# A lead of 52 instead of 48 row maxima in a fused Fourier mixing and attention kernel

## The chip, the cores and the metric

The kernel runs on one core of a Trainium2 chip. The metric is device time in microseconds (us) of one execution. The core's engines run side by side, each on its own instruction stream: PE (TensorE) does the matmuls, DVE (VectorE), ACT (ScalarE) and POOL (GpSimd) do the element work, SP's queue issues most transfers. They meet through semaphores only.

## The reference

The input x has 2048 rows (S) of 512 (D). Two branches are mixed row by row by a gate:

```python
g = _sigmoid((x * gate_w).sum(-1, keepdims=True))
# branch a: real part of a two-dimensional DFT, as dense matrices
a = jnp.einsum("bsd,ed->bse", x, dft_hid_re)
b = jnp.einsum("bsd,ed->bse", x, dft_hid_im)
y = jnp.einsum("ts,bse->bte", dft_seq_re, a) - jnp.einsum("ts,bse->bte", dft_seq_im, b)
# branch b: attention with H = 32 heads of 16
q, k, v = qkv[0], qkv[1], qkv[2]
scores = jnp.einsum("bhqd,bhkd->bhqk", q, k) * scale
p = _softmax(scores, axis=-1)
o = jnp.einsum("bhqk,bhkd->bhqd", p, v)      # then o @ wo
return g * y + (1 - g) * (o @ wo)
```

All is float32. Products that need the precision are made of three: each operand is split into a high and a low part, and high x high, high x low and low x high are summed.

## The kernel before

**Two halves of PE.** Most operands have at most 64 rows of contraction, so the kernel keeps the upper and the lower 64 rows of the array busy with two different matmuls at a time. A *slot* is one such place in the order: one matmul on either half.

**The softmax needs row maxima first.** Heads are handled in 16 pairs; head 0 of a pair lives in rows 0 to 63 of the stacks `qs` and `ks`, head 1 in rows 64 to 127. Each stack exists twice, and pair p uses number p % 2. `load_stacks(p)` (L202 to L211) fills the two stacks of a pair from DRAM by twelve DMAs of 128 KB in SP's queue, the six of head 0 first. A *maxima tile* (`a_tile`, L217) multiplies 128 query rows with 512 keys (L223), and DVE reduces the result to one maximum per row (L225). A pair has 64 such tiles per head. When a block of them is complete, `m_parts` and `m_rows` (L233, L242) split the negated maxima and write them by eight small DMAs (L248, four from SP and four from POOL) into two further rows of `qs`. A *score* (`scores`, L727) then multiplies 50 rows (L741), so that the maximum is subtracted by the matmul itself, and ACT takes the exponential (L742). `pv` (L767) multiplies the result with the values (L777) for two units (a unit is 128 keys of one pair and half of the queries).

**The maxima run ahead of the scores.** The distance is `LEAD` (L26), 48 tile indices for each head. It is built before the scores begin. `four` (L307) makes the products of four row tiles at a time for V and for the imaginary part of the hidden DFT; it has four phases of twelve product slots, and after the slots 3 and 8 of each phase it adds a pair of maxima tiles, one per head (L323, `maxima`).

**The long middle stage** is a written order of *sections*. A section is one string of slots and ends with `|`, the value matmuls of two units. In a string `s` is a score, `a` a maxima tile, both on one half, while the other half gets a product of the DFT (L429); a two-letter slot has a score or tile on both halves and no product. Head 1's first letters stand in the even sections, head 0's in the odd ones. 24 sections are THIN, 192 are FULL (16 slots, eight scores and eight maxima tiles). The last 32 sections with the output projection as the other work are FOURTEEN (8 pairs of sections), NINE (3), TEN, TWELVE, TEN, TWELVE, TEN; their names and what they hold:

```python
FULL = "s a s s a a s s a a s a s a a s |"
NINE = "aS s a s a ^ sA a a s a s sA |", "aS a s s a ^ sA a s a s s aS sA |"
FOURTEEN = "s a s a sS ^ a s s a s a aA |", "aS s a a s ^ s a sS s a s a sA |"
TWELVE = ("sA a s a s ^ s a s a s s a s |",) * 2
TEN = "aA s s a s ^ s s s a a sS |", "a s a sS a ^ s s s s s aA |"
```

A pair of sections holds 16 maxima tiles in NINE, 14 in FOURTEEN, 12 in TWELVE, 10 in TEN. `^` and the end of a section take one deferred step of the maxima.

**What sets the order of the loads.** Transfers that don't belong to a DFT chain are called by a plan (`at`, `run_plan`) at the end of a section by the number of units whose values are done: `load_stacks(p)` at unit 32 (p - 1) - 1, when the last scores that read the same buffers, pair p - 2's, have just been issued. In SP's queue stand, among others, the chunks of the DFT matrix (`craw`, L364), the row of a finished chain (`yr`, L483), the blocks of attention output (`oh<-nh`, L570, which waits for POOL) and these loads (L210, L211), in the order of the program.

**The first rows** of the real part are made by `four` too, while the first scores are taken (L971 to L983); `real_next` (L443) copies each of four results to a tile `y`, of which there are two. **The start** has eight matmuls on zeros (L157 to L160) before the first loads arrive. **The end**: `LastPair.products` (L688) makes the last four row blocks; block 0 is finished by ACT and POOL, the others by DVE (L609), and each is stored by one DMA (L700).

Of the kernel before, what the change touches and what calls it, by code (L numbers as in the profile page):

```python
# [22 lines left out]
KT = D // P  # L23
NT = S // P
UNITS = NP * 32
LEAD = 48  # L26
RAW = 6
PSUM = bass.MemoryType.PSUM
DRAM = bass.MemoryType.DRAM
# [3 lines left out]
def mix_kernel(ctx: ExitStack, tc: tile.TileContext, xa_t, xa, wqkv, w_hid, w_seq, wo, gate_w, out):  # L33
# [5 lines left out]
    nc = tc.nc  # L39
# [5 lines left out]
    const = ctx.enter_context(tc.tile_pool(name="const", bufs=1))  # L45
# [10 lines left out]
    oh_d = [[dram.tile([P, 2, S // 2], F32, name=f"oh{hf}{ct}") for ct in range(3)] for hf in range(2)]  # L56
    r_d = [[dram.tile([2, 4, S // 2], F32, name=f"r{hf}{ct}") for ct in range(4)] for hf in range(2)]

    ident = const.tile([P, P], F32, name="ident")
    make_identity(nc, ident)  # L60

# [5 lines left out]
    omg = const.tile([P, NT], F32, name="omg")  # L67
# [5 lines left out]
    xab = [const.tile([P, 4, 2, D], F32R, name=f"xab{tb}", tag=f"xab{tb}") for tb in range(4)]  # L73
# [22 lines left out]
    wch = st1.tile([P, KT, D], F32R, name="wch")  # L96
    wcl = st1.tile([P, KT, D], F32R, name="wcl")
# [32 lines left out]
    with tc.tile_pool(name="qk", bufs=1, reuse_waits="tile") as pool:  # L130
        wh = pool.tile([P, 2, KT, D], F32R, name="wh")
        wl = pool.tile([P, 2, KT, D], F32R, name="wl")

        def mm_qk(ps, c, ct, tb, kt):
            cols = slice(ct * P, (ct + 1) * P)
            x = xab[tb][:, :, :, kt * P:(kt + 1) * P]
            mm3(ps, wh[:, c, kt, cols], wl[:, c, kt, cols], x[:, :, 0], x[:, :, 1], kt == 0, kt == KT - 1)

        def evac_qk(ps, c, ct, tb):
            hl = pool.tile([P, 2, D], F32R, name="hl", bufs=7)  # L140
            hi_lo(hl[:, 0], hl[:, 1], ps)
            nc.sync.dma_start(qk_d[c][:, ct * P:(ct + 1) * P, tb * 512:(tb + 1) * 512].rearrange("v p t -> p v t"),
                              hl.bitcast(F32))

        for kt in range(KT):
            add(wh[:, 0, kt], wl[:, 0, kt], wqkv[0, :, kt], nc.vector)
            add_x(0, kt)
        for kt in range(KT):
            add(wh[:, 1, kt], wl[:, 1, kt], wqkv[1, :, kt], nc.vector)
        for tb in range(1, 4):  # L150
            for kt in range(KT):
                add_x(tb, kt)
        for kt in range(KT):
# [3 lines left out]
        nc.vector.memset(wch[:, 0].bitcast(F32), 0.0)  # L157
        ps = turn_of("f")
        for _ in range(8):
            nc.tensor.matmul(ps, wch[:, 0, :P], wch[:, 0], start=True, stop=True)  # L160
        split(8)

        xgs = {}

        def gate_row(s):

            xg = xgs.pop(s)
            nc.vector.scalar_tensor_tensor(xg, xg, 1.0, gwb, op0=ALU.mult, op1=ALU.mult, accum_out=z[:, s:s + 1])
            if s + 5 < NT:
                xgs[s + 5] = staged(xa[s + 5])  # L170

        for tb in range(4):
            if tb == 2:
                assert not todo and not loaded
                nc.sync.dma_start(gwb, gate_w.broadcast_to([P, D]))
                xgs.update({s: staged(xa[s]) for s in range(5)})
            for c in range(2):
                if tb == 0 and c == 0:
                    pss = [turn_of("f") for _ in range(4)]
                    for kt in range(KT):  # L180
                        for ct in range(4):
                            mm_qk(pss[ct], c, ct, tb, kt)
                    split(4)
                    for ct in range(4):
# [83 lines left out]
    ab = [xab[s // 4][:, s % 4] for s in range(NT)]  # L268
# [35 lines left out]
        a_next += 1  # L304
        return users[1]

    def four(ss, wh, wl, done, between=None):  # L307

        ps = [turn_of("s") for _ in ss]
        seen = None  # L310
        for phase, pair in enumerate(((0, 1), (2, 3), (1, 0), (3, 2))):
            guard, seen = seen, None
            both = [row_products(ss[c], wh, wl) for c in pair]
            for j in range(12):
                for half, c in enumerate(pair):
                    st, mv = next(both[half])
                    r = slice(64 * half, 64 * half + 64)
                    i = nc.tensor.matmul(ps[c], st[r], mv[r], start=phase < 2 and j == 0, stop=phase > 1 and j == 11)  # L318
                    if phase > 1 and j == 0:
                        tc.add_manual_dep(  # L320
                            i.ins, guard.ins.name,
                            mybir.DependencyInfo(mybir.DependencyClass.Sync, mybir.DependencyReason.DATA))
                if j in (3, 8):  # L323
                    user = between(phase, j) if between else maxima()
                    seen = seen or user
            if deferred:
                deferred.pop(0)()
            if phase > 1:
                for c in sorted(pair):
                    done(ss[c], ps[c])  # L330

    for s in range(8):
        ps = turn_of("s")
# [11 lines left out]

    wre = [[const.tile([P, D], F32R, name=f"wre{v}{kt}", tag=f"w{4 * v + kt}") for kt in range(KT)] for v in range(2)]
    for s in range(0, NT, 4):
        four(range(s, s + 4), [wch[:, kt] for kt in range(KT)], [wcl[:, kt] for kt in range(KT)], b_done)
    run_deferred()
    assert a_next == LEAD  # L350
    right.__exit__(None, None, None)
# [88 lines left out]
                yield chain, h1, wre[1][kt], None  # L440
                yield chain, l1, wre[0][kt], partial(real_next, s, t, chain) if kt == KT - 1 else None

    def real_next(s, t, chain):  # L443
        y = work.tile([P, D], F32, name="y", bufs=2)
        nc.scalar.copy(y, chain.ps)  # L445
# [52 lines left out]
    oh, yp, wos = {}, {}, []  # L498
# [100 lines left out]

    few, by_others = [], set()  # L600

    def finish(ps, t, y, other=False):
        if other:

            tmp = few[0][:, t % 4]
            nc.scalar.activation(tmp, ps, AF.Copy, scale=omg[:, t:t + 1])
            nc.gpsimd.tensor_tensor(y, y, tmp, ALU.add)
            return
        nc.vector.scalar_tensor_tensor(y, ps, omg[:, t:t + 1], y, op0=ALU.mult, op1=ALU.add)  # L609

# [41 lines left out]
    class LastPair:  # L652
# [35 lines left out]
        def products(self, others):  # L688

            pss = [o_bank() for _ in range(4)]  # L690
            for i, (st, mv) in enumerate(((0, 0), (0, 1), (1, 0))):
                for c in range(4):
                    r = slice(32 * c, 32 * c + 32)
                    nc.tensor.matmul(pss[c], self.o15[r, st], w15[0][r, mv], start=i == 0, stop=i == 2)
            for c in sorted(range(4), key=lambda c: c not in others):
                t = 8 + 4 * self.blk + c
                finish(pss[c], t, yp[t], c in others)
            for c in range(4):
                t = 8 + 4 * self.blk + c
                (nc.scalar if c in others else nc.sync).dma_start(out[t * P:(t + 1) * P, :], yp.pop(t))  # L700

    last_pairs = []

# [169 lines left out]

    FULL = "s a s s a a s s a a s a s a a s |"
    THIN = "aS s a s a s s a s a s a a sA |"
    NINE = "aS s a s a ^ sA a a s a s sA |", "aS a s s a ^ sA a s a s s aS sA |"
# [91 lines left out]
    run_plan(0)  # L968
    gate()

    def first_rows(s, ps):  # L971
# [72 lines left out]
```

## Time and profile before

| what | value |
|---|---|
| median of 3 runs | 1681.99 us (1681.66 to 1682.1) |
| profiled execution, its own time | 1682.39 us |
| its span, first to last instruction | 1680.6 us |
| mean granted TensorE clock | 0.999 |
| 345 to 1450 us (THIN's end and FULL): busy PE, DVE, ACT, POOL | 1104.99, 952.77, 883.19, 562.21 of 1105.00 |
| 1456 to 1577 us (FOURTEEN and NINE) | 120.69, 105.87, 100.08, 32.27 of 121.00 |
| 1577 to 1640 us (TEN and TWELVE) | 62.80, 49.93, 55.98, 22.85 of 63.00 |

The profile belongs to one execution, so sums of its rows are compared with that execution's own time, 1682.39 us. A matmul's length in it runs until its result has left the array; neighbours overlap, and the pace is the distance between starts. L777 counts 16 matmuls at a section's end, since each of the eight of the program is recorded as two.

### The profile page before, as it was taken

How to read it: one execution, taken by the hardware profiler on the slowest of the kernel's cores; microseconds unless marked ns; L12 is line 12 of the kernel's file. 1: busy time of each engine (PE TensorE's matmuls, PEld its weight loads, DVE VectorE, ACT ScalarE, POOL GpSimd, SP SyncE). 2: the span in 40 equal slices, each digit the busy share in tenths (PEclk: the TensorE clock that was granted, in tenths of full speed). 3: DMA queues.
4: the chain of work that ended last, by engine and by line, in shares of the span. 5: the costliest groups of instructions: out<-in, count | busy, mean ns of one | idle time of the engine just before them, and what ended most of it. 6: DMA issues, size and time to landing. Idle time of an engine off the chain costs nothing.

```text
span 1680.6 us, 34603 instructions
## 1 busy us (share of the span) xinstructions
PE 1670.8 (99%) x13120; PEld 1016.6 (60%) x13120; DVE 1378.1 (82%) x2297; ACT 1245.8 (74%) x2469; POOL 750.9 (45%) x813
## 2 busy tenths in 40 slices
PE   9999999999999999999999999999999999999998
PEld 7888766655555555555555555555555555555554
DVE  5448688888888888888888888888888888888885
ACT  5212288877777888778877788777877788788886
POOL 0214634544444466445444466454554465322231
PEclk9999999999999999999999999999999999999999
DMA  9963500314141432414165533423241535731014
GB/s 294 341 155 108 178 13 14 52 45 83 45 84 46 83 101 85 83 46 89 39 145 190 103 108 89 96 55 73 64 89 46 103 102 108 273 66 34 26 40 134
DMA packets 82622, 165.16 MB, mean 98 GB/s; under 512 B 19904, under 2 KB 20168, under 8 KB 78616
## 3 DMA queue, kind: packets, MB, share of 16 engines
q1 hardware_dynamic: 77832, 162.30, 37.2%
q8 instruction: 103, 1.69, 0.4%
q0 software_dynamic: 4480, 0.39, 0.3%
q14 instruction: 63, 0.52, 0.1%
q10 hardware_dynamic: 144, 0.26, 0.0%
HBM read 107.73 MB, written 54.52 MB: 97 GB/s over the span
## 4 chain that ended last, share of the span: by engine, by line
PE 98%; POOL 1%; DVE 1%; issue 0%; DMA 0%; SPq 0%; ACT 0%; DVEq 0%; POOLq 0%; ACTq 0%
PE d L429 40%; PE t L777 27%; PE t L223 11%; PE t L741 7%; PE t L318 4%; PE t L90 2%; PE t L89 2%; PE t L91 2%; PE t L336 1%; PE t L758 1%; PE t L429 1%; DVE mx L225 0%; PE d L223 0%; PE t L160 0%; POOL hl L295 0%
## 5 line engine op out<-in xcount | busy, mean ns | idle before, releaser
L225 DVE TENSOR_REDUCE mx<-t 128x1 f32<-128x512 f32 x2022 | 1255.6, 684 | 211.1 <-PE t L223 173.4
L742 ACT ACTIVATE pt<-t 128x512 f32<-128x512 f32 x2048 | 1034.1, 629 | 10.1 <-PE t L741 9.9
L741 PE MATMUL t<-qs,ks 50*128 50x512 f32 x2048 | 741.6, 409 | 0.8 <-ACT y L445 0.5
L223 PE MATMUL t<-ks,qs 48*128 48x512 f32 x2022 | 690.4, 400 | 0.1
L429 PE MATMUL d<-xab,ch 64*128 64x512 f32 x2016 | 657.5, 401 | 0.0
L777 PE MATMUL t<-pt,vt 128*32 128x512 f32 x3968 | 477.1, 598 | 0.2
L429 PEld LDWEIGHTS d<-xab,ch 64*128 64x128 f32 x2016 | 357.7, 184 | 132.9 <-issue 98.9
L223 PEld LDWEIGHTS t<-ks,qs 48*128 48x128 f32 x2022 | 367.7, 185 | 80.2 <-ACT pt L742 42.0
L741 PEld LDWEIGHTS t<-qs,ks 50*128 50x128 f32 x2048 | 370.4, 185 | 67.1 <-DVE mx L225 37.9
L429 PE MATMUL d<-xab,cl 64*128 64x512 f32 x1008 | 403.6, 400 | 0.0
L792 POOL TENSOR_TENSOR osum<-osum,oe 128x512 f32<-128x512 f32 x217 | 279.7, 1289 | 161.0 <-ACT oe L786 154.1
L786 ACT COPY oe<-t 128x512 f32<-128x512 f32 x217 | 127.5, 588 | 230.6 <-PE t L777 228.2
L777 PEld LDWEIGHTS t<-pt,vt 128*32 128x32 f32 x3968 | 103.8, 109 | 231.2 <-issue 148.4
L374 POOL CAST ch<-craw 128x512 fp32r<-128x512 f32 x126 | 77.4, 615 | 351.4 <-PE t L741 291.6
L429 PEld LDWEIGHTS d<-xab,cl 64*128 64x128 f32 x1008 | 185.7, 184 | 67.8 <-issue 51.1
L375 POOL TENSOR_TENSOR cl<-craw,ch 128x512 fp32r<-128x512 f32 x126 | 162.5, 1290 | 10.2
L248 POOL DMA_DIRECT2D qs<-mt x132 | 74.3, 568 | 77.7 <-DVE mt L244 72.6
L429 PE MATMUL d<-wo_hl,o_hl 64*128 64x512 f32 x288 | 77.3, 395 | 0.0
L429 PE MATMUL d<-wre,xab 64*128 64x512 f32 x288 | 70.4, 389 | 0.0
L429 PEld LDWEIGHTS d<-wo_hl,o_hl 64*128 64x128 f32 x288 | 52.2, 185 | 13.4 <-DVE yp L609 5.0
L429 PEld LDWEIGHTS d<-wre,xab 64*128 64x128 f32 x288 | 52.9, 185 | 3.9 <-DVE mx L225 0.3
L89 PE MATMUL t<-xab,wh 128*128 128x512 f32 x128 | 50.2, 392 | 0.0
(123 smaller groups left out, 913.1 us busy)
## 6 DMA issues: line engine op xcount, KB each, us to landing
craw<-w_seq SPq DMA_DIRECT2D x128, 256.0 KB
qk<-hl SPq DMA_DIRECT2D x32, 512.0 KB
qs<-qk SPq DMA_DIRECT2D x96, 128.0 KB
ks<-qk SPq DMA_DIRECT2D x96, 128.0 KB
b<-hl SPq DMA_DIRECT2D x16, 512.0 KB
xab<-b SPq DMA_DIRECT2D x16, 512.0 KB
o<-osum SPq DMA_DIRECT2D x62, 128.0 KB
oh<-nh SPq DMA_DIRECT2D x12, 512.0 KB
```

The costliest lines, as they stand in the source:

```text
L89: nc.tensor.matmul(ps, sh, mh, start=first, stop=False)
L223: nc.tensor.matmul(ps, qs[p % 2][r, qt * P:(qt + 1) * P], ks[p % 2][r, kb * 512:(kb + 1) * 512], start=True, stop=True)
L225: user = nc.vector.tensor_reduce(mx[p % 2][:, h, qt, kb:kb + 1], ps, AX.X, ALU.max)
L248: (nc.sync, nc.gpsimd)[h].dma_start(rows.rearrange("v (q b c) -> v b q c", q=n, b=4)[:, b], mt[k % 2][32 * b + h:32 * b + 4 * n:2])
L374: nc.gpsimd.tensor_copy(h1, raw)
L375: nc.gpsimd.tensor_tensor(l1, raw, h1.bitcast(F32), ALU.subtract)
L429: i = nc.tensor.matmul(self.ps, st[r], mv[r], start=not self.begun, stop=stop)
L741: nc.tensor.matmul(ps, ks[p % 2][rr, kt * P:(kt + 1) * P], qs[p % 2][rr, q0:q0 + 512], start=True, stop=True)
L742: return nc.scalar.activation(pts[u][:, 2 * qb + h], ps, AF.Exp, bias=0.0, scale=DH ** -0.5)
L777: nc.tensor.matmul(acc[32 * j:32 * j + 32], vt[:, kt, p, h:h + 32], pt[:, j], start=u == us[0], stop=u == us[-1])
L786: nc.scalar.copy(oe, acc)
L792: nc.gpsimd.tensor_tensor(o, o, oe, ALU.add)
```

## The change

`LEAD` is 52. In the four groups of the imaginary rows, one phase of each (the second) has three pairs of maxima tiles instead of two. Every maxima tile of the later stream stands four indices earlier, beside the same scores. The late sections hold eight tiles fewer: NINE is gone, and there are FOURTEEN (11 pairs of sections), TEN (3), TWELVE, TEN. Four smaller edits: the matmuls on zeros read a tile of their own, set before anything else on DVE, and are ten; the first twelve products are ordered by operand (high x high of all four, then the low weights, then the low x); the four `y` of the first rows have four places; the last row block is finished and stored in two halves, by two queues, and block 0's ACT and POOL work is cut in two.

```diff
-LEAD = 48
+LEAD = 52
...
+    zero = const.tile([P, P], F32R, name="zero", tag="zero")
+    nc.vector.memset(zero.bitcast(F32), 0.0)
     ident = const.tile([P, P], F32, name="ident")
...
-        nc.vector.memset(wch[:, 0].bitcast(F32), 0.0)
         ps = turn_of("f")
-        for _ in range(8):
-            nc.tensor.matmul(ps, wch[:, 0, :P], wch[:, 0], start=True, stop=True)
+        for _ in range(10):
+            nc.tensor.matmul(ps, zero, zero.unsqueeze(1).broadcast_to([P, 4, P]), start=True, stop=True)
...
-                    for kt in range(KT):
+                    for w, v in ((wh, 0), (wl, 0), (wh, 1)):
+                        for ct in range(4):
+                            nc.tensor.matmul(pss[ct], w[:, c, 0, ct * P:(ct + 1) * P], xab[tb][:, :, v, :P],
+                                             start=w is wh and not v, stop=False)
+                    for kt in range(1, KT):
...
-                if j in (3, 8):
+                if j in ((2, 5, 9) if three and phase == 1 else (3, 8)):
...
-        four(range(s, s + 4), [wch[:, kt] for kt in range(KT)], [wcl[:, kt] for kt in range(KT)], b_done)
+        four(range(s, s + 4), [wch[:, kt] for kt in range(KT)], [wcl[:, kt] for kt in range(KT)], b_done, three=True)
...
-    def real_next(s, t, chain):
-        y = work.tile([P, D], F32, name="y", bufs=2)
+    def real_next(s, t, chain, y=None):
+        if y is None:
+            y = work.tile([P, D], F32, name="y", bufs=2)
...
-            tmp = few[0][:, t % 4]
-            nc.scalar.activation(tmp, ps, AF.Copy, scale=omg[:, t:t + 1])
-            nc.gpsimd.tensor_tensor(y, y, tmp, ALU.add)
+            for c in range(n):
+                cols = slice(c * D // n, (c + 1) * D // n)
+                tmp = few[0][:, t % 4, cols]
+                nc.scalar.activation(tmp, ps[:, cols], AF.Copy, scale=omg[:, t:t + 1])
+                nc.gpsimd.tensor_tensor(y[:, cols], y[:, cols], tmp, ALU.add)
...
-                finish(pss[c], t, yp[t], c in others)
+                halves = [slice(0, D // 2), slice(D // 2, D)] if self.blk and c == 3 else [slice(0, D)]
+                for cols in halves:
+                    finish(pss[c][:, cols], t, yp[t][:, cols], c in others, 2)
...
-        for patterns, n in ((FOURTEEN, 8), (NINE, 3), (TEN, 1), (TWELVE, 1), (TEN, 1), (TWELVE, 1), (TEN, 1)):
+        for patterns, n in ((FOURTEEN, 11), (TEN, 3), (TWELVE, 1), (TEN, 1)):
...
-        real_next(s, ab[s], chain)
+        if s % 2 == 0:
+            first_y.append(work.tile([P, 2, D], F32, name="y01", tag=("no", "nh")[s // 2]))
+        real_next(s, ab[s], chain, first_y[-1][:, s % 2])
```

The lines of the changed kernel are a few higher: L223, L429, L741 and L777 are L228, L434, L756 and L792 there.

**Where the stream of maxima reaches the stacks of pair 10.** This is PE's order before, inside the even section that follows the value matmuls at 1049.64 us of the profile (L223 is a maxima tile of head 1, L741 a score, L429 a DFT product; `qs1` and `ks1` are pair 9's stacks, `qs0` and `ks0` pair 10's):

```order
L223 MATMUL t_14730<-ks1_937,qs1_935 128x512
L429 MATMUL d_14534<-xab2_177,ch_14498 128x512
L223 MATMUL t_14734<-ks1_937,qs1_935 128x512
L429 MATMUL d_14534<-xab2_177,ch_14498 128x512
L741 MATMUL t_14738<-qs1_935,ks1_937 128x512
L429 MATMUL d_14534<-xab2_177,cl_14499 128x512
L223 MATMUL t_14742<-ks1_937,qs1_935 128x512
```

and this is the same place of the changed kernel:

```order
L228 MATMUL t_14755<-ks1_940,qs1_938 128x512
L434 MATMUL d_14559<-xab2_179,ch_14523 128x512
L228 MATMUL t_14759<-ks0_939,qs0_937 128x512
L434 MATMUL d_14559<-xab2_179,ch_14523 128x512
L756 MATMUL t_14763<-qs1_938,ks1_940 128x512
L434 MATMUL d_14559<-xab2_179,cl_14524 128x512
L228 MATMUL t_14767<-ks0_939,qs0_937 128x512
```

The fifth maxima tile of the section is the first that reads pair 10's stacks; before, head 1 came to them two sections later, after its first score there. The section with the call of the loads is the same in both, three sections ahead. So it is for each pair from 1 to 14.

**A phase of the imaginary rows.** PE's order before, from the first slots of the second phase of the first group (L318 is a product, x2 and x4 are one and two slots on both halves; L223 a maxima tile):

```order
L318 MATMUL t<-wcl,xab_175 128x512 x2
L318 MATMUL t<-wch,xab_175 128x512 x4
L223 MATMUL t<-ks_936,qs_934 128x512 x2
L318 MATMUL t<-wcl,xab_175 128x512 x2
L318 MATMUL t<-wch,xab_175 128x512 x4
L318 MATMUL t<-wcl,xab_175 128x512 x2
L318 MATMUL t<-wch,xab_175 128x512 x2
L223 MATMUL t<-ks_936,qs_934 128x512
L223 MATMUL d<-ks_936,qs_934 128x512
```

and in the changed kernel:

```order
L323 MATMUL t<-wcl,xab_177 128x512 x2
L323 MATMUL t<-wch,xab_177 128x512 x2
L228 MATMUL t<-ks_939,qs_937 128x512 x2
L323 MATMUL t<-wch,xab_177 128x512 x2
L323 MATMUL t<-wcl,xab_177 128x512 x2
L323 MATMUL t<-wch,xab_177 128x512 x2
L228 MATMUL t<-ks_939,qs_937 128x512
L228 MATMUL d<-ks_939,qs_937 128x512
L323 MATMUL t<-wch,xab_177 128x512 x2
L323 MATMUL t<-wcl,xab_177 128x512 x2
L323 MATMUL t<-wch,xab_177 128x512 x4
L228 MATMUL t<-ks_939,qs_937 128x512 x2
```

The phase has a third pair of maxima tiles, and so one slot more.

More of the change, by code (lines that the diff above doesn't have):

```diff
@@ L305, in maxima, with four @@
         return users[1]
-    def four(ss, wh, wl, done, between=None):
+    def four(ss, wh, wl, done, between=None, three=False):
         ps = [turn_of("s") for _ in ss]
@@ L600, in mix_kernel, with finish @@
     few, by_others = [], set()
-    def finish(ps, t, y, other=False):
+    def finish(ps, t, y, other=False, n=1):
         if other:
-            tmp = few[0][:, t % 4]
-            nc.scalar.activation(tmp, ps, AF.Copy, scale=omg[:, t:t + 1])
-            nc.gpsimd.tensor_tensor(y, y, tmp, ALU.add)
+            for c in range(n):
[3 more added lines that the diff above has]
+                nc.gpsimd.tensor_tensor(y[:, cols], y[:, cols], tmp, ALU.add)
             return
@@ L696, in products @@
                 t = 8 + 4 * self.blk + c
-                finish(pss[c], t, yp[t], c in others)
+                halves = [slice(0, D // 2), slice(D // 2, D)] if self.blk and c == 3 else [slice(0, D)]
+                for cols in halves:
+                    finish(pss[c][:, cols], t, yp[t][:, cols], c in others, 2)
             for c in range(4):
                 t = 8 + 4 * self.blk + c
-                (nc.scalar if c in others else nc.sync).dma_start(out[t * P:(t + 1) * P, :], yp.pop(t))
+                y = yp.pop(t)
+                if self.blk and c == 3:
+                    nc.scalar.dma_start(out[t * P:(t + 1) * P, :D // 2], y[:, :D // 2])
+                    nc.sync.dma_start(out[t * P:(t + 1) * P, D // 2:], y[:, D // 2:])
+                else:
+                    (nc.scalar if c in others else nc.sync).dma_start(out[t * P:(t + 1) * P, :], y)
     last_pairs = []
@@ L875, in mix_kernel @@
     THIN = "aS s a s a s s a s a s a a sA |"
-    NINE = "aS s a s a ^ sA a a s a s sA |", "aS a s s a ^ sA a s a s s aS sA |"
     FOURTEEN = "s a s a sS ^ a s s a s a aA |", "aS s a a s ^ s a sS s a s a sA |"
@@ L969, in mix_kernel @@
     gate()
+    first_y = []
     def first_rows(s, ps):
```

## The prediction

> **What bounds the kernel now.** I read the page's busy times and chain of waits first, then PE's timeline in the long middle stage, then the timeline of SP's queue beside it.
>
> ```profile
> PE 1670.8 (99%) x13120; PEld 1016.6 (60%) x13120; DVE 1378.1 (82%) x2297; ACT 1245.8 (74%) x2469; POOL 750.9 (45%) x813
> PE 98%; POOL 1%; DVE 1%; issue 0%; DMA 0%; SPq 0%; ACT 0%; DVEq 0%; POOLq 0%; ACTq 0%
> ```
>
> PE is busy for 99% of the span and carries 98% of the chain. It takes its matmuls in program order, so every microsecond for which one of them waits in the middle stage is added to the end; there is no idle time in which it could be won back. So the question is whether the change makes a matmul wait. Pair 10 shows where to look:
>
> ```profile
> 1049.64 1.92 PE L777 MATMUL t<-pt,vt 128*32 128x512 f32 x16
> ...
> 1053.47 0.39 PE L223 MATMUL t<-ks,qs 48*128 48x512 f32 x1
> ...
> 1053.70 0.39 PE L223 MATMUL t<-ks,qs 48*128 48x512 f32 x1
> ...
> 1061.26 1.92 PE L777 MATMUL t<-pt,vt 128*32 128x512 f32 x16
> ...
> 1063.45 0.40 PE L223 MATMUL t<-ks,qs 48*128 48x512 f32 x1
> ```
>
> The columns are start, length, engine and line. L777 closes a section; two sections take 1061.26 - 1049.64 = 11.62 us, one 5.81. Two neighbouring slots (1053.47 and 1053.70) start 0.23 us apart. By the order before, the row at 1063.45 is the first maxima tile of head 1 on the stacks of pair 10, and the one at 1053.70 is the tile four earlier. These are the loads of those stacks, in SP's queue:
>
> ```profile
> 1045.15 0.59 SPq L570 DMA_DIRECT2D oh<-nh  x1
> 1045.83 0.55 SPq L210 DMA_DIRECT2D qs<-qk  x1
> ...
> 1047.74 0.42 SPq L211 DMA_DIRECT2D ks<-qk  x1
> ...
> 1050.37 0.30 SPq L210 DMA_DIRECT2D qs<-qk  x1
> 1051.35 0.30 SPq L211 DMA_DIRECT2D ks<-qk  x1
> 1052.55 0.30 SPq L210 DMA_DIRECT2D qs<-qk  x1
> 1053.53 0.30 SPq L211 DMA_DIRECT2D ks<-qk  x1
> ```
>
> There are twelve loads, head 0's six and then head 1's. The program gives its transfers eight semaphores in turn, so from the ninth on an issue waits until the transfer eight before it has landed. The issue at 1053.53 therefore marks the landing of the fourth load, issued at 1047.74 (5.8 us). The last four issues are (1053.53 - 1050.37)/3 = 1.05 us apart, which is the pace of the landings, so the twelfth lands 8 x 1.05 = 8.4 us after its issue, near 1061.9. Head 1's first tile at 1063.45 has 1.5 us to spare.
>
> **The lead of 52.** The new order puts the first tile of pair 10, head 1, exactly where the row at 1053.70 stands, 9.75 us earlier. The loads are not called earlier: their place is tied to the value sections, and the buffers are read by pair 8's scores until just before. PE then waits from 1053.70 until the landing, 8 us. The same two rows, last load issued and place of the new first tile, for pairs 4, 6, 7, 9, 13 and 14:
>
> ```profile
> 489.50 0.30 SPq L211 DMA_DIRECT2D ks<-qk  x1
> 495.80 0.39 PE L223 MATMUL t<-ks,qs 48*128 48x512 f32 x1
> 678.85 0.30 SPq L211 DMA_DIRECT2D ks<-qk  x1
> 681.72 0.39 PE L223 MATMUL t<-ks,qs 48*128 48x512 f32 x1
> 769.56 0.30 SPq L211 DMA_DIRECT2D ks<-qk  x1
> 774.65 0.39 PE L223 MATMUL t<-ks,qs 48*128 48x512 f32 x1
> 950.92 0.30 SPq L211 DMA_DIRECT2D ks<-qk  x1
> 960.69 0.39 PE L223 MATMUL t<-ks,qs 48*128 48x512 f32 x1
> 1328.32 0.30 SPq L211 DMA_DIRECT2D ks<-qk  x1
> 1332.69 0.39 PE L223 MATMUL t<-ks,qs 48*128 48x512 f32 x1
> 1421.67 0.30 SPq L211 DMA_DIRECT2D ks<-qk  x1
> 1426.25 0.39 PE L223 MATMUL t<-ks,qs 48*128 48x512 f32 x1
> ```
>
> With a landing 8.2 us after the last issue (a little under pair 10's 8.4) the waits are 1.9, 5.3, 3.1, 8.0 (pair 10), 3.8 and 3.6 us, together 25.7. Pair 9 just escapes: 959.1 against 960.69. The pairs not shown read alike and have more to spare than it. The six are those whose loads sit late in SP's queue: for 6, 10 and 14 behind the store of L570, which waits for POOL, for 4, 7, 10 and 13 behind the result row of a finished DFT chain. Neither depends on the lead. What is queued behind the waiting tile is the rest of the section: ACT gets no scores, DVE no tiles, and both only run dry. The bounds: a landing after 5.8 us, the fourth load's time, leaves 0, 2.9, 0.7, 5.6, 1.4 and 1.2 = 11.8 us; a microsecond more for each gives 31.7. I take 25.7, since the twelfth has seven others ahead of it in flight.
>
> **PE after a long wait.** How PE runs after 8 us of idleness no row shows. The nearest is its start:
>
> ```profile
> 2.17 3.78 PE L160 MATMUL t<-wch 128*128 128x512 f32 x8 [2.17 <-DVE wch L157]
> 5.75 0.69 PE L89 MATMUL t<-xab,wh 128*128 128x512 f32 x1
> ...
> 7.74 0.39 PE L90 MATMUL t<-xab,wh 128*128 128x512 f32 x1
> ...
> 209.19 0.49 PE L741 MATMUL t<-qs,ks 50*128 50x512 f32 x1 [0.54 <-ACT y L445]
> ```
>
> Twelve matmuls start between 2.17 and 7.74, in 5.57 us, where 12 x 0.23 = 2.8 would do: a cold start costs some 2.6 us beside a short wait. After the 0.54 us of idleness at 209.19 the pace is full at once. So the cost is between 0 and 6 x 2.6 = 15.6 us. I take one cold start, 2.6 us, for the wait of pair 10, which is by far the longest. The Trainium skill (TensorE: Matmul & The Clock Gate, Part 1: The HAM clock gate) states that the array drops to half its clock after an idle window of about 3.4 us; the slow start agrees, four of my six waits are longer than that, and the term would be 10.4 us by the rule.
>
> **The early phases.** Four maxima pairs are added there, each one slot on both halves: 4 x 0.23 = +0.9 us. DVE has six reductions in such a phase instead of four and rests in the phases beside it, with four banks between, so I let PE not wait for it; if that cover were gone it would be 0.3 us a phase, +2.1 in all.
>
> **The late sections.** Pairs of sections by their closing rows, first fourteen maxima (FOURTEEN), then NINE's sixteen, then TWELVE and TEN:
>
> ```profile
> 1532.87 1.92 PE L777 MATMUL t<-pt,vt 128*32 128x512 f32 x16
> 1543.63 0.64 PE L777 MATMUL t<-pt,vt 128*32 128x512 f32 x4
> 1554.94 1.92 PE L777 MATMUL t<-pt,vt 128*32 128x512 f32 x16
> 1566.24 1.06 PE L777 MATMUL t<-pt,vt 128*32 128x512 f32 x8
> ...
> 1587.59 1.92 PE L777 MATMUL t<-pt,vt 128*32 128x512 f32 x16
> 1597.84 1.92 PE L777 MATMUL t<-pt,vt 128*32 128x512 f32 x16
> 1607.40 1.06 PE L777 MATMUL t<-pt,vt 128*32 128x512 f32 x8
> ...
> 1585.67 0.39 PE L429 MATMUL d<-wo_hl,o_hl 64*128 64x512 f32 x1
> 1586.27 0.46 PE L741 MATMUL t<-qs,ks 50*128 50x512 f32 x1 [0.20 <-DMA qs<-mt]
> ```
>
> FOURTEEN takes 10.76, NINE 11.30, TWELVE 10.25, TEN 9.56. Three NINE become FOURTEEN (-1.6) and one TWELVE becomes TEN (-0.7). The last two rows are neighbours: the score at 1586.27 waited for rows of maxima and began 0.60 us after its neighbour instead of 0.23; these rows come half a section sooner: -0.4. Together -2.7.
>
> **The smaller parts.** The score at 209.19 waited 0.54 us for a copy that needed one of two y buffers; with four there is no such wait: -0.6 with its slot. The warm-up needs no longer DVE's second instruction and may begin 1 us sooner, half of which is gained while PE is slow: -0.5 (0 to -1.1). In the tail, halves of the last row block are finished and stored apart:
>
> ```profile
> 1674.05 2.07 DVE L609 SCALAR_TENSOR_TENSOR yp<-t,omg,yp 128x512 f32<-128x512 f32 x3 [0.17 <-PE t L694]
> ```
>
> One such pass is 0.69 us. At best one leaves the end, at worst a half pass is added; the last stores queue behind each other, so I take 0 (-0.7 to +0.4).
>
> **The sum**, on the profiled execution's own 1682.4: +25.7 + 2.6 + 0.9 - 2.7 - 0.6 - 0.5 = 1707.8. That execution lies 0.4 above the median of the runs shown, 1681.99, so I forecast 1707.
>
> **The rivals.** (a) Each of the four longest waits is followed by a cold start (the rule above): 3 x 2.6 = 7.8 more, 1715. For it speaks only the start's rows; against it, that no row shows how long PE must rest.
> (b) The late loads land as fast as the fourth did, 5.8 us after the issue: 11.8 of waits, 1694. Against it stands the steady 1.05 us between the last issues.
> (c) The other side: the loads keep ahead of the earlier tiles. It would take pair 10's last load issued before 1053.70 - 8.2 = 1045.5, eight microseconds sooner, and with it that POOL frees the queue at L570 so much sooner, because the maxima rows that SP writes (L248) now stand farther ahead of it. Then only the gains and the early slots stay, 1682.0 + 0.9 - 2.7 - 0.6 - 0.5 = 1679. Against it: by the order those writes stood ahead of the loads before, too, and the row at 1045.15 is held by POOL's own work.
> (d) The change isn't what it says: excluded, as the order shows each part.
>
> **The numbers.** I give my forecast 0.70 (with its own range 1701 to 1712), (a) 0.12, (b) 0.09, (c) 0.06, and 0.03 to a loss from elsewhere. The range 1696 to 1716 holds the first two and the edge of the third. About 0.2% (3.4 us) is what a measurement of this kernel tells from no change. Only (c) is faster; (b) with yet faster landings could reach no change: faster 0.06, same 0.03, slower 0.91.
>
> **What would show it.** In the changed profile PE idles before the first maxima tile of pairs 4, 6, 7, 10, 13 and 14, released by a DMA of ks or qs, near 8 us for pair 10 and 2 to 5 for the others, and hardly at all for 9; the middle sections are otherwise 5.81 us; matmuls run slow for some microseconds after pair 10's wait; the late pairs take 10.76 and 9.56. I am wrong if those tiles start without a wait, or if the time stands below 1690.

## The result and the profile after

| | before | after |
|---|---|---|
| median of 4 runs each | 1681.83 us (1681.49 to 1682.1) | 1717.84 us (1717.13 to 1722.48) |
| ratio, after to before | | 1.022 (1.0208 to 1.0232) |
| profiled execution, its own time | 1682.39 us | 1722.48 us |
| its span | 1680.6 us | 1720.5 us |
| its mean granted TensorE clock | 0.999 | 0.987 |

The change made the kernel 36 us slower. That is 10.8 us more than forecast and 1.8 us above the end of the range. The profiled execution is the slowest of the four; the other three, 1717.13 to 1718.02 us, ran at a granted clock of 0.989 to 0.990.

The page of the changed kernel, first the busy times, then the chain by engine, then the group of maxima tiles (line, engine, shapes, count, busy time and mean ns, idle time of PE just before it and what ended most of it):

```profile
PE 1684.8 (98%) x13122; PEld 1023.1 (59%) x13122; DVE 1378.9 (80%) x2298; ACT 1247.7 (73%) x2470; POOL 752.7 (44%) x814
PE 93%; DMA 5%; SPq 1%; DVE 1%; issue 0%; DVEq 0%
L228 PE MATMUL t<-ks,qs 48*128 48x512 f32 x2020 | 695.0, 403 | 27.7 <-DMA ks<-qk 16.3
```

DMA has entered the chain with 5% of the span, and PE has waited 27.7 us before maxima tiles. PE's timeline shows where; these are head 1's first tiles of pairs 4, 6, 7, 10, 13 and 14 (start, length, engine, line; the idle time before each and what ended it in brackets):

```profile
498.12 0.47 PE L228 MATMUL t<-ks,qs 48*128 48x512 f32 x1 [2.98 <-DMA craw<-w_seq]
691.04 0.76 PE L228 MATMUL t<-ks,qs 48*128 48x512 f32 x1 [5.21 <-DMA craw<-w_seq]
789.89 0.76 PE L228 MATMUL t<-ks,qs 48*128 48x512 f32 x1 [3.00 <-DMA craw<-w_seq]
1080.10 0.76 PE L228 MATMUL t<-ks,qs 48*128 48x512 f32 x1 [8.43 <-DMA ks<-qk]
1366.21 0.76 PE L228 MATMUL t<-ks,qs 48*128 48x512 f32 x1 [4.13 <-DMA ks<-qk]
1466.06 0.76 PE L228 MATMUL t<-ks,qs 48*128 48x512 f32 x1 [3.78 <-DMA ks<-qk]
```

Three of them name a load of `craw` as the releaser, which the tile does not read: transfers take semaphores in turn, and the profile names the event that came last. That the loads of the stacks are the cause is seen from the nearly constant time between their last issue and the tile (below), from the landing of that load, and from the experiments. SP's queue has the last load of each of the six pairs here:

```profile
489.45 0.30 SPq L216 DMA_DIRECT2D ks<-qk  x1
683.24 0.30 SPq L216 DMA_DIRECT2D ks<-qk  x1
781.75 0.30 SPq L216 DMA_DIRECT2D ks<-qk  x1
1071.21 0.30 SPq L216 DMA_DIRECT2D ks<-qk  x1
1357.62 0.30 SPq L216 DMA_DIRECT2D ks<-qk  x1
1457.45 0.30 SPq L216 DMA_DIRECT2D ks<-qk  x1
```

From the last issue to the start of the tile it takes 8.67, 7.80, 8.14, 8.89, 8.59 and 8.61 us. The last event on that load's own semaphore comes 8.53, 7.55, 7.83, 8.58, 8.45 and 8.47 us after the issue: the tile starts 0.14 to 0.31 us after the landing, in all six.

What follows a wait is in PE's busy time and granted clock, in stretches of 3.41 us cut where the clock changes. A row has the stretch and its length, the busy time of PE, of its weight loads, of DVE, ACT and POOL (in brackets the instructions), the granted clock (the share of full speed at which PE's clock ran), and the DMA engines' busy share and GB/s. First the stretch in which the wait of pair 4 lies and two after it, then the same for pair 6 with one more, then one for pair 7:

```profile
495.20:498.61 3.41, 0.49 (x4) 0.51 (x6) 0.92 (x2) 0.79 (x2) 0.00 (x0) 1.00 0.82 234
498.61:502.03 3.42, 3.42 (x21) 1.95 (x22) 2.80 (x5) 1.79 (x3) 0.26 (x2) 0.50 0.01 4
502.03:505.44 3.41, 3.41 (x34) 2.04 (x28) 1.31 (x3) 1.90 (x4) 0.26 (x2) 1.00 0.00 0
686.34:689.75 3.41, 0.00 (x0) 0.00 (x0) 0.47 (x1) 0.34 (x1) 0.00 (x0) 1.00 0.86 149
689.75:693.17 3.42, 2.13 (x10) 1.90 (x12) 1.17 (x2) 0.60 (x1) 0.00 (x0) 0.50 0.39 137
693.17:696.58 3.41, 3.41 (x18) 1.03 (x20) 1.63 (x4) 1.19 (x2) 0.42 (x2) 0.50 0.02 5
696.58:700.00 3.42, 3.42 (x32) 2.39 (x24) 1.93 (x4) 2.53 (x6) 1.57 (x2) 1.00 0.00 0
785.33:788.74 3.41, 1.55 (x14) 1.01 (x10) 2.52 (x4) 2.41 (x5) 1.29 (x1) 1.00 0.93 180
788.74:792.15 3.41, 2.26 (x10) 1.97 (x12) 1.30 (x2) 0.72 (x2) 0.00 (x0) 0.50 0.27 102
```

PE is just as busy from 693.17 to 696.58 as from 696.58 to 700.00, but it gets through 18 instructions in the first of the two and 32 in the second: in the first the clock is at half. All six waits are followed by half clock, the short ones of 2.98 (pair 4) and 3.00 us (pair 7) as well.

**Where the 40.1 us of the profiled execution went** (1722.48 - 1682.39). From one section's value matmuls to the next takes 5.81 us where nothing is wrong. The twelve sections with the six waits and behind them exceed that by 43.8 us in all. Of these 28.6 are the waits (start of the tile less that of its neighbour in the order, less 0.23: 3.15, 5.38, 3.17, 8.60, 4.30, 3.95). The other 15.2 us are matmuls at half clock, 1.6 us (pair 4) to 3.0 (pair 13) for each wait. The late sections take 2.5 us less, the time to the end of THIN 0.3 less, some small waits of the middle stage 1.1 less, and the tail the same; 0.2 lie outside the span.

### The profile page after: what moved, and what is told of

It is laid out like the page before. It is cut to its first block, busy times and chain, and to the rows that moved or that the text cites. A ratio compares the mean times of both kernels' runs of the same rounds, so it can differ in the third digit from the quotient of the medians.

```text
span 1720.5 us, 34595 instructions
## 1 busy us (share of the span) xinstructions
PE 1684.8 (98%) x13122; PEld 1023.1 (59%) x13122; DVE 1378.9 (80%) x2298; ACT 1247.7 (73%) x2470; POOL 752.7 (44%) x814
## 4 chain that ended last, share of the span: by engine, by line
PE 93%; DMA 5%; SPq 1%; DVE 1%; issue 0%; DVEq 0%
PE d L434 36%; PE t L792 26%; PE t L228 11%; PE t L756 7%; PE t L323 5%; DMA ks<-qk 3%; PE t L93 2%; PE t L91 2%; PE t L92 2%; PE t L341 1%; PE t L773 1%; DMA craw<-w_seq 1%; PE t L434 1%; DMA qs<-qk 0%; DVE mx L230 0%; SPq L216 0%
## 5 line engine op out<-in xcount | busy, mean ns | idle before, releaser
L756 PE MATMUL t<-qs,ks 50*128 50x512 f32 x2048 | 741.4, 411 | 0.0
L228 PE MATMUL t<-ks,qs 48*128 48x512 f32 x2020 | 695.0, 403 | 27.7 <-DMA ks<-qk 16.3
L434 PE MATMUL d<-xab,ch 64*128 64x512 f32 x2016 | 663.9, 404 | 0.0
L792 PE MATMUL t<-pt,vt 128*32 128x512 f32 x3968 | 483.4, 605 | 0.3
L434 PEld LDWEIGHTS d<-xab,ch 64*128 64x128 f32 x2016 | 361.7, 186 | 133.1 <-issue 100.1
L228 PEld LDWEIGHTS t<-ks,qs 48*128 48x128 f32 x2020 | 370.3, 187 | 108.8 <-ACT pt L757 41.5
L756 PEld LDWEIGHTS t<-qs,ks 50*128 50x128 f32 x2048 | 371.4, 186 | 63.6 <-DVE mx L230 36.9
L434 PE MATMUL d<-xab,cl 64*128 64x512 f32 x1008 | 406.8, 404 | 0.0
L792 PEld LDWEIGHTS t<-pt,vt 128*32 128x32 f32 x3968 | 104.5, 110 | 237.2 <-issue 152.4
L434 PEld LDWEIGHTS d<-xab,cl 64*128 64x128 f32 x1008 | 187.4, 186 | 67.8 <-issue 50.5
L434 PE MATMUL d<-wo_hl,o_hl 64*128 64x512 f32 x288 | 77.6, 396 | 0.0
L434 PE MATMUL d<-wre,xab 64*128 64x512 f32 x288 | 70.2, 389 | 0.0
L434 PEld LDWEIGHTS d<-wo_hl,o_hl 64*128 64x128 f32 x288 | 52.1, 185 | 17.3 <-DVE yp L617 8.4
L244 POOL CAST nhl<-nm 128x16 fp32r<-128x16 f32 (+1 forms) x33 | 6.5, 197 | 119.0 <-DVE nm L241 119.0
L434 PEld LDWEIGHTS d<-wre,xab 64*128 64x128 f32 x288 | 52.8, 185 | 4.0 <-DVE mx L230 0.3
```

The lines of the kernel that those rows point to most:

```text
L228: nc.tensor.matmul(ps, qs[p % 2][r, qt * P:(qt + 1) * P], ks[p % 2][r, kb * 512:(kb + 1) * 512], start=True, stop=True)
L434: i = nc.tensor.matmul(self.ps, st[r], mv[r], start=not self.begun, stop=stop)
L756: nc.tensor.matmul(ps, ks[p % 2][rr, kt * P:(kt + 1) * P], qs[p % 2][rr, q0:q0 + 512], start=True, stop=True)
L792: nc.tensor.matmul(acc[32 * j:32 * j + 32], vt[:, kt, p, h:h + 32], pt[:, j], start=u == us[0], stop=u == us[-1])
```

## The experiments

**The two parts of the change, each alone.** First the kernel before with only the lead of 52:

```diff
-LEAD = 48
+LEAD = 52
...
-                if j in (3, 8):
+                if j in ((2, 5, 9) if three and phase == 1 else (3, 8)):
...
-        for patterns, n in ((FOURTEEN, 8), (NINE, 3), (TEN, 1), (TWELVE, 1), (TEN, 1), (TWELVE, 1), (TEN, 1)):
+        for patterns, n in ((FOURTEEN, 11), (TEN, 3), (TWELVE, 1), (TEN, 1)):
```

> The kernel before with only the lead of 52: the third pair in one phase of each group and the late sections with FOURTEEN (11), TEN (3), TWELVE, TEN; the zero matmuls, first products, y buffers and last stores as before. My theory, that the loss is all the lead's (waits of 28.6 us before head 1's first tiles and some 15 us of half clock behind them): the same six waits, and 1717.8 + 1 to 1.5 for the gains of the small edits that are now missing = 1718 to 1720 us. Rival, that the small edits have a part in the slow clock or the loss: below 1715.

It took 1719.23 us (1715.69 to 1722.07; 1.0222, 1.0207 to 1.0238). The six waits are there, and the loss is the lead's. Its runs differ by 6 us, and they follow the granted clock: 1722.07 us at 0.987, 1715.69 at 0.991. Its trace has a shorter wait than any of the changed kernel's, at pair 4. PE's timeline, then its busy time and clock around it and behind the wait of pair 13:

```profile
498.66 0.76 PE L223 MATMUL t<-ks,qs 48*128 48x512 f32 x1 [2.09 <-DMA craw<-w_seq]
```

```profile
495.10:498.51 3.41, 1.48 (x14) 0.87 (x10) 2.46 (x4) 2.35 (x5) 1.26 (x1) 1.00 0.89 217
498.51:501.92 3.41, 3.26 (x14) 2.33 (x14) 2.13 (x4) 1.19 (x2) 0.00 (x0) 0.50 0.11 40
501.92:505.33 3.41, 3.41 (x32) 1.79 (x31) 1.39 (x4) 1.93 (x4) 0.42 (x2) 1.00 0.00 0
...
1365.50:1368.91 3.41, 3.05 (x14) 2.33 (x14) 1.93 (x3) 1.19 (x2) 0.00 (x0) 0.50 0.94 282
1368.91:1372.32 3.41, 3.41 (x18) 0.60 (x16) 0.87 (x3) 0.60 (x1) 1.63 (x3) 0.50 0.33 97
```

Here even 2.09 us of idleness are followed by half clock.

Then the changed kernel with the lead put back, so that only the four small edits are left (the diff above, the other way round, in the changed kernel):

> The changed kernel with its lead put back to 48, two pairs in every phase and the late sections of before; only the four small edits are left. My theory: no wait before head 1's first tiles, clock 0.99 or more, and the gains that the prediction gave them, 0.6 for the y buffers and 0.5 for the zero matmuls, nothing for the tail: 1682 - 1.1 = 1680.9 (1680 to 1682). Rival, that an edit costs time: above 1682.5.

1680.17 us (1679.94 to 1680.74) beside 1681.73 for the kernel before, 0.9991 (0.9981 to 1.0): together the edits cost no time and gain some 1.6 us, which the interval hardly tells from nothing. What each does alone was not measured. No wait stands before head 1's first tiles.

**Keeping PE busy through the waits.** If PE's rest is what halves the clock, work without use in the wait must bring the clock back and leave the wait:

```diff
+        if h == 1 and j == 0:
+            for _ in range({4: 12, 6: 21, 7: 12, 10: 35, 13: 17, 14: 15}.get(p, 0)):
+                nc.tensor.matmul(ps, zero, zero.unsqueeze(1).broadcast_to([P, 4, P]), start=True, stop=True)
         nc.tensor.matmul(ps, qs[p % 2][r, qt * P:(qt + 1) * P], ks[p % 2][r, kb * 512:(kb + 1) * 512],
```

> The changed kernel with matmuls on the tile of zeros put into the wait before head 1's first tile of pairs 4, 6, 7, 10, 13 and 14 (12, 21, 12, 35, 17 and 15 of them at 0.23 us, each set a little shorter than its wait), written to the tile's own bank and overwritten by it. My theory, that PE's rest of 3.1 us or more is what brings the half clock and costs 15 us on top of the waits: the waits stay as a stretch without useful work, the granted clock stays at 1, 1717.8 - 15 + 0.5 = 1703 (1701 to 1706). Rival 1, that the slow stretch belongs to the late loads themselves (their transfers or the DVE and ACT that ran dry): half clock or stalls remain, 1715 to 1720. Rival 2, that four of six waits are what matters: some 1707.

It took 1707.36 us (1706.73 to 1707.7), the profiled execution 1706.73. PE's timeline at pair 10, then busy time and clock:

```profile
1063.91 8.23 PE L230 MATMUL t<-zero 128*128 128x512 f32 x35
1072.59 0.47 PE L231 MATMUL t<-ks,qs 48*128 48x512 f32 x1 [0.45 <-issue]
```

```profile
1068.00:1072.00 4.00, 4.00 (x19) 3.09 (x17) 0.00 (x0) 0.00 (x0) 0.00 (x0) 1.00 0.84 128
1072.00:1076.00 4.00, 3.55 (x31) 1.83 (x30) 2.61 (x5) 1.72 (x3) 0.20 (x1) 1.00 0.47 178
```

The loads are as late as before, DVE, ACT and POOL have run just as dry (their three figures of 0.00 in the first row), and the clock stays at 1.00. The six sections exceed 5.81 us by 28.4 us together: the waits are all there, and the extra of 15.2 us is gone. So rival 1 falls: the slow stretches come from PE's rest and not from the late loads or the starved engines. The time misses my 1703. I had taken 15 us, the profiled execution's cost, off the median of all runs; between the two profiled executions the difference is 15.75 us (1722.48 - 1706.73), between the two medians 10.5 (1717.84 - 1707.36). The cost of the half clock differs from run to run. By medians it is near rival 2's 1707; that the cost came from four waits alone is excluded by the changed kernel's trace, in which all six have it. The other three runs left no trace, so which of their waits had it is not known.

**How short a rest is enough.** The same kernel with fewer zero matmuls, so that a rest of a chosen length stays before each tile:

```diff
-            for _ in range({4: 12, 6: 21, 7: 12, 10: 35, 13: 17, 14: 15}.get(p, 0)):
+            for _ in range({4: 8, 6: 16, 7: 4, 10: 25, 13: 10, 14: 11}.get(p, 0)):
```

> The kernel with zero matmuls in the waits, with fewer of them, so that PE rests before the first tile of pair 4 for about 1.0 us, pair 14 1.25, pair 6 1.5, pair 13 1.75, pair 7 2.0 and pair 10 2.5. It asks how short a rest brings the half clock; a rest of 2.1 us brought it once in the kernel with the lead alone, and 0.5 us did not. Theory 1, that a rest must fill about half of one step of the clock record (3.4 us): no drop up to 1.5, a drop at 2.5, between them by chance; 1709 to 1713 us. Theory 2, that any rest over 1 us brings it: all six, 1715 to 1719. Theory 3, that it takes a rest of about 3.4 us as a whole: none, 1707.

1707.59 us (1707.42 to 1708.83). The rests of pairs 7, 10, 13 and 14 by PE's timeline (those of 4 and 6 came out at 0.45 and 0.43 us), then busy time and clock around pairs 7 and 10:

```profile
783.79 0.47 PE L231 MATMUL t<-ks,qs 48*128 48x512 f32 x1 [1.86 <-DMA qs<-qk]
...
1071.45 0.47 PE L231 MATMUL t<-ks,qs 48*128 48x512 f32 x1 [2.58 <-DMA qs<-qk]
...
1356.29 0.47 PE L231 MATMUL t<-ks,qs 48*128 48x512 f32 x1 [1.23 <-DMA o<-osum]
...
1453.26 0.47 PE L231 MATMUL t<-ks,qs 48*128 48x512 f32 x1 [1.08 <-DMA craw<-w_seq]
```

```profile
782.52:785.93 3.41, 2.14 (x18) 1.54 (x22) 1.63 (x3) 1.30 (x3) 0.00 (x0) 1.00 0.38 114
785.93:789.35 3.42, 3.42 (x32) 1.94 (x26) 2.07 (x5) 2.11 (x5) 0.42 (x2) 1.00 0.00 0
...
1069.24:1072.65 3.41, 1.20 (x10) 1.15 (x12) 0.69 (x2) 0.46 (x1) 0.00 (x0) 1.00 1.00 284
1072.65:1076.06 3.41, 3.41 (x18) 0.98 (x20) 1.92 (x4) 1.26 (x3) 0.42 (x2) 0.50 0.05 17
```

Only the rest of 2.58 us brought half clock, and for one stretch of 3.41 us; 1.08, 1.23 and 1.86 did not. Theories 2 and 3 fall in this execution. Theory 1 holds for the pattern, but its time was 1.4 us too high, since most rests came out shorter than I had set them and one stretch at half clock costs no more than 1.7 us, half of 3.41. The rest of 1.86 us is spread over two stretches (783.79 - 1.86 = 781.93, and a stretch ends at 782.52), so these rows do not say what it does inside one.

**Head 1's loads sooner.** Head 1 has its last score on the old stacks one section before head 0, by the order of FULL. So its six loads need not wait for head 0's:

```diff
-    def load_stacks(p):
+    def load_stacks(p, hs=(0, 1)):
...
-        for h in range(2):
+        for h in hs:
...
-        at(32 * (p - 1) - 1, load_stacks, p)
+        at(32 * (p - 1) - 3, load_stacks, p, (1,))
+        at(32 * (p - 1) - 1, load_stacks, p, (0,))
```

> The changed kernel with the loads of head 1's stacks called one section (5.8 us) sooner than head 0's, which stay where they are. My theory: head 1's six loads are then issued by some 1042 us for pair 10 and have landed by 1052, ahead of their first tile; the six waits and all half clock go, and the lead's small terms are left: 1682 - 2.5 (late sections) - 0.3 (early part, net) = 1679 (1678 to 1681). Rival, that the loads wait for something else at the new place (the last scores of pair p - 2 on head 1, or a craw load ahead of them): waits stay at some pairs, 1685 to 1705.

1693.78 us (1.0073, 1.0058 to 1.0088). The six waits are gone, but two others have come, before scores, where the stacks of pair 2 and of pair 15 are loaded:

```profile
297.41 0.80 PE L756 MATMUL t<-qs,ks 50*128 50x512 f32 x2 [5.94 <-DMA ks<-qk]
...
1508.76 0.80 PE L756 MATMUL t<-qs,ks 50*128 50x512 f32 x2 [5.53 <-DMA ks<-qk]
```

These are the last scores of pairs 0 and 13. The sections there are THIN and FOURTEEN, in which head 1 has scores in the odd section too, so that the scores came behind the new loads in the order, waited for them and read the new stacks in place of the old. So this kernel does not compute the reference, and its time says nothing of the idea as a whole. The fault was mine; for pairs 3 to 14 the waits are gone. The rival's 1685 to 1705 holds the time, and it named these last scores, but as what the loads would wait for; here the scores waited for the loads. The next kernel, with the same argument `hs`, moves the loads of pairs 3 to 14 alone:

```diff
...
-        at(32 * (p - 1) - 1, load_stacks, p)
+        early = 2 < p < 15
+        at(32 * (p - 1) - (3 if early else 1), load_stacks, p, (1,) if early else (0, 1))
+        if early:
+            at(32 * (p - 1) - 1, load_stacks, p, (0,))
```

> The changed kernel with head 1's six loads called one section sooner for pairs 3 to 14 alone. For pairs 2 and 15 all twelve stay where they are: in THIN and FOURTEEN head 1 has its last scores on the old stacks in the odd section, so that there the early loads of the kernel before this one came too soon, overwrote stacks that were still to be read, and cost two waits of 6.4 and 6.0 us. My theory: none of the six waits, no half clock in the middle, and the lead's own terms alone: 1680.2 (the small edits alone) - 2.1 (late sections) + 1.3 (early part) = 1679.4 us (1678.5 to 1680.5), faster than the kernel before and level with or a little under the small edits alone. Rival, that head 0's six loads, still behind POOL's store, now come late to their own first tiles: a wait of some us at pair 10, 1683 or more.

1678.21 us (1677.65 to 1678.7) beside 1681.27 for the kernel before, 0.998 (0.9972 to 0.9989): 3.1 us or 0.2% less than the kernel before, clear of one by the interval, and 1.2 us under my figure. Some 1.6 us of that the small edits gain without the lead, so that only about 1.5 us is left for the lead itself, and the two kernels were measured on different chips. No run has the early loads with a lead of 48. PE is busy for 1668.7 us, 100% of the span. The group of maxima tiles on its page:

```profile
L228 PE MATMUL t<-ks,qs 48*128 48x512 f32 x2020 | 687.9, 399 | 0.1
```

The idle time before maxima tiles is 0.1 us where the changed kernel had 27.7, for both heads: the rival's wait at head 0's first tiles is not there. In SP's queue at pair 10 head 1's first and last load now stand ahead of the store that POOL holds up, and head 0's first behind it:

```profile
1031.77 0.33 SPq L215 DMA_DIRECT2D qs<-qk  x1
...
1033.99 0.42 SPq L216 DMA_DIRECT2D ks<-qk  x1
...
1045.28 0.58 SPq L576 DMA_DIRECT2D oh<-nh  x1
1045.95 0.56 SPq L215 DMA_DIRECT2D qs<-qk  x1
```

**Only the order of the twelve turned round**, head 1's six first:

```diff
-    def load_stacks(p):
+    def load_stacks(p, hs=(1, 0)):
...
-        for h in range(2):
+        for h in hs:
```

> The changed kernel with the order within the twelve loads turned round: head 1's six first, then head 0's. My theory, that what is late is the place in the queue: head 1's six land about 3 us sooner, and head 0's, now the last, are wanted half a section (some 3.5 us) after head 1's first tile. Waits fall from 28.6 to some 5 to 10 us (pair 10 keeps about 4, pair 6 about 2), and with one to three slow stretches the time is 1685 to 1692. Rival, that all twelve land together whatever their order: waits of head 1 stay, above 1705.

1685.41 us (1684.07 to 1686.61; 1.0026, 1.0015 to 1.0036), at the lower edge of what the theory gave: the waits of the profiled execution, the fastest of the eight, are 4.6 us together, a little under the 5 to 10 expected, and it has no slow stretch in the middle. PE's timeline has the two waits left at pair 10, head 1's first and then head 0's (at pair 6 there is one of 0.32 us), and its busy time and clock show the stretches over which they lie:

```profile
1055.17 0.46 PE L228 MATMUL t<-ks,qs 48*128 48x512 f32 x1 [2.09 <-DMA ks<-qk]
...
1061.53 0.47 PE L228 MATMUL t<-ks,qs 48*128 48x512 f32 x1 [2.17 <-issue]
```

```profile
1053.65:1057.06 3.41, 1.89 (x18) 1.54 (x22) 1.80 (x4) 1.42 (x3) 0.00 (x0) 1.00 1.05 123
1057.06:1060.47 3.41, 2.30 (x19) 0.55 (x18) 1.22 (x3) 1.68 (x3) 0.42 (x2) 1.00 0.94 106
1060.47:1063.89 3.42, 2.36 (x20) 2.29 (x22) 1.86 (x3) 1.63 (x4) 0.00 (x0) 1.00 0.79 265
```

The place in the queue of the loads is what was late. The wait of 2.09 us, the same length as that of pair 4 in the kernel with the lead alone, brought no half clock here: each of the two waits is spread over two stretches, and PE is busy for more than half of each of them (1.89 of 3.41 us at the least).

**The kernel before with all loads a section later** (lead 48):

```diff
-        at(32 * (p - 1) - 1, load_stacks, p)
+        at(32 * (p - 1) + 1, load_stacks, p)
```

> The kernel before (lead 48) with every load_stacks called one section (5.8 us) later. It asks whether the waits follow from the spare time alone, without the lead. In the kernel before, the last load lands by my reckoning 1.75 us ahead of its first tile for pair 10 and 4.45 us for pair 6, and 6 us or more for the others; less 5.8 us that gives waits of about 4.1 and 1.4 us, and, as the loads also leave behind other neighbours in the queue, up to 2 us either way. With one or two slow stretches: 1686 to 1692. Rival, that the lead itself (more tiles on DVE, other neighbours) makes the loads late: no wait, 1682.

1690.3 us (1687.82 to 1690.89; 1.005, 1.0037 to 1.0064): the time is in my range, but the reasons are others. At pair 10 PE was idle for 0.64 us and not for 4, at pair 6 not at all. Pair 10's loads no longer come right behind POOL's store, and their last is issued at 1062.09 us; the program is 6.6 us later there by the tile's own place, so that against 1053.53 before the shift is 2.0 us and not 5.8. The largest wait stands before a score at 603.61, 14.6 us after the last load of pair 5's stacks was issued (589.01); PE's row, and POOL's row that leads to it:

```profile
603.61 0.79 PE L741 MATMUL t<-qs,ks 50*128 50x512 f32 x1 [3.54 <-ACT oe L786]
```

```profile
598.00 0.61 POOL L374 CAST ch<-craw 128x512 fp32r<-128x512 f32 x1 [13.97 <-DMA craw<-w_seq]
```

The loads had moved to just ahead of a chunk of the DFT matrix in SP's queue, which was issued at 590.15 and landed at 598.00; POOL waited 13.97 us for it, was late with the sums of attention output behind it, ACT's next copy of such a sum came late, and the score waited for that copy. So the time is in the range by luck, and the kernel does not decide the question it was made for. The traces of the kernel before and of the changed kernel answer it more directly: from the issue of the last load of those six pairs to its landing it took 8.17 us in the mean in the one and 8.24 in the other. So the lead does not slow the loads; its tiles come sooner. What this kernel shows is that "spare time less the shift" is no way to size a move in a queue that holds its neighbours up.

## Why the prediction was wrong, and where it was right

- **The lead of 52, the waits: right.** Six waits were forecast, at pairs 4, 6, 7, 10, 13 and 14, and none at 9; these six came and no other. Their sum is 28.6 us against 25.7. The step that gave the size was "a landing 8.2 us after the last issue", and it held: the landing came after 8.24 us in the mean (7.55 to 8.58). Left out was that the tile starts 0.21 us behind the landing in the mean; from last issue to tile it was 8.45, which makes 1.5 of the 2.9 us. Most of the rest is that the last issues stood up to 0.8 us later against the tiles than before (pair 4's tile would have started at 494.97, 5.5 us behind its last load's issue at 489.45; in the prediction's rows it was 495.80 - 489.50 = 6.3).
- **PE after a long wait: wrong, and the larger of the two misses that took the time out of the range.** The step was "I take one cold start, 2.6 us, for the wait of pair 10". There were six, 15.2 us together in the profiled execution, 2.5 each in the mean, near the term's upper bound of 15.6. By medians, as the kernel with the zero matmuls shows, it is 10.5. Of the 10.8 us by which the median was missed, 10.5 - 2.6 = 7.9 come from this step and 2.9 from the waits; either alone would have left the time below 1716. I had chosen the low value because no row of before showed how long PE must rest. What was open was the count, and there I let "by far the longest" decide with no row for it. That 2.6 is near the mean of 2.5 is partly luck: the six starts cost 1.6 to 3.0 us, and the price at the kernel's start varies too (in the changed kernel and in the one with chosen rests PE begins at 1.06 us, and its clock rises at 7.09 and at 4.28). Between one and six the wide end of the range had to hold six: 1707 + 13 = 1720.
- **Rival (a), the Trainium skill's rule** (TensorE: Matmul & The Clock Gate, Part 1: The HAM clock gate), stood nearest: four restarts, 1715. That its 10.4 us are the 10.5 of the medians is luck, since in the trace the two short waits were followed by half clock as well. The page speaks of a window of about 3.4 us that runs freely and does not begin with the kernel's work; the trace agrees, as all changes of the clock lie multiples of 3.41 us apart. It also says that the clock falls after one idle window or more. I had read that as a wait of 3.4 us; here the clock fell in stretches of which PE was idle for only a part, and so after waits of 2.98, 3.00 and, in other kernels, 2.58, 2.54 and once 2.09 us too.
- **The smaller terms: right in sum.** Late sections -2.5 against -2.7 (pairs of FOURTEEN by their closing rows 10.83 us and of TEN 9.57, below); the small edits -1.6 by medians against -1.1; the early phases +0.65 to +1.4, by the end of THIN in the kernels with and without the lead, against +0.9; the tail 0.
- **Rivals (b), (c) and (d)** did not occur. The six loads' landing, 7.55 us after the issue at the least, excludes the 5.8 of (b), and none of the six kept ahead. Its 1694 lay outside the range of 1696 to 1716, which was said to hold its edge.

The late sections' closing rows in PE's timeline after, two of FOURTEEN two sections apart, and two of TEN:

```profile
1542.47 1.93 PE L792 MATMUL t<-pt,vt 128*32 128x512 f32 x16
...
1553.30 1.92 PE L792 MATMUL t<-pt,vt 128*32 128x512 f32 x16
...
1618.55 1.92 PE L792 MATMUL t<-pt,vt 128*32 128x512 f32 x16
...
1628.12 1.06 PE L792 MATMUL t<-pt,vt 128*32 128x512 f32 x8
```

## What to carry to other kernels

When work is moved earlier, find the transfers that feed it and what releases their buffers: here a lead of four tiles cost 36 us because the loads stayed where they were, and with six loads called a section sooner the same lead cost nothing and may have gained a microsecond or two. A wait of the matmul engine is not paid with its own length alone; count a stretch at half clock for every wait above some 2 us (of two waits of 2.09 us here one brought it and one did not, and all from 2.54 us on did), not for the longest only, and where the count is unknown let the range hold all of them. Before a call is moved, see in every kind of section it falls into which readers of the old data still stand behind it.

## What was not expected of the hardware

- In every kept trace the granted clock changes only on a grid of 3.41 us. In the middle of the kernels it fell at the end of stretches in which PE was idle for 52% (1.76 of 3.41 us, pair 7 of the lead alone), 54% (1.86, pair 7 of the changed kernel), 57% (1.93, pair 4 of the lead alone), 65% (2.21, the chosen rests) and more, and did not fall after 37% (part of the rest of 1.86 us) and 45% (1.52, the reversed order). That about half a stretch decides is read from these rows and was not tried by itself.
- It rose again at the end of the first stretch in which PE was nearly always busy: 3.26 of 3.41 us were enough (pair 4 of the lead alone), 3.05 were not (pair 13 there), nor 2.13 (pair 6 of the changed kernel). So in the profiled execution a wait of 3 to 9 us cost, beside its length, half of the time at half clock that lay behind it, up to the second step of the grid after its end. The runs of the same kernel lie some 5 us apart and follow the granted clock; that this comes from where the waits fall on the grid fits the traces but is not shown, since only one run of each kernel left one.
